# Half of the heads write their small products to the other rows of a second PSUM bank

## The chip, the cores and the metric

The kernel runs on one core of one Trainium2 chip. The metric is the device time of one execution, in microseconds (us); the time of a version is the median of its runs. The core's engines are TensorE (PE in the profile, its weight loads PEld), VectorE (DVE), ScalarE (ACT), GpSimd (POOL) and SyncE (SP), which issues the transfers.

## The reference

A delta-rule attention over 768 steps for 4 batches of 8 heads of width 48, and a feed-forward layer with a mish-like gate on its output.

```python
k_n = k / (np.linalg.norm(k, axis=-1, keepdims=True) + 1e-06)
for t in range(S):
    y[:, :, t] = einsum('bhd,bhde->bhe', q[:, :, t], state)
    v_old = einsum('bhde,bhd->bhe', state, k_n[:, :, t])
    state = state + beta[t] * einsum('bhd,bhe->bhde', k_n[:, :, t], v[:, :, t] - v_old)
x = y.transpose(0, 2, 1, 3).reshape(3072, 384)
h = x @ w_in                                  # 384 x 2048
g = h * np.tanh(np.log1p(np.exp(h)))          # h itself above 20
out = g @ w_out                               # 2048 x 384
```

## The kernel before

The 768 steps are cut into 12 chunks (n) of C = 64 steps. The 32 pairs of batch and head are 16 (NP) pairs p of two batch halves hh; hh = 0 and 1 lie on rows 0 to 63 and 64 to 127 of the tiles. The heads are also cut in two halves h of 8 (PB), and those in quarters h4 of four. Within a chunk the recurrence becomes matrix products: KK^T of the keys, the inverse T of a triangular 64x64 matrix made from it, Z~ = T times the values less K S, and y from Z~, Q and the state S.

Everything is written as stages, small Python generators, that are put on one plan with a time each (`put`, `at`, `defer`, and the table `TN`); the plan is run in order of these times. Up to plan time 90 the scheduler orders all engines; after it TensorE's instructions stay in the plan's order, and the scheduler orders the others. The stages on TensorE are:

- `early(g)`, for a group g of two chunks: the keys are transposed (kt, L267), KK^T goes to pg (L286), the masked part to d on VectorE (L289) and the rest to at on ScalarE (L291). VectorE then transposes d to gt (L297), makes the norms, and solves for the 32x32 diagonal blocks of T by 30 steps of two instructions each (pr at L345, gt at L347). In groups 0 and 1 16x16 blocks are solved, and `merge` joins them (ma, mb).
- `s_a` and `s_b` (ta, tb): the products of 32x32 blocks that give the off-diagonal block of T. Their copies go to at (L457) and tt (L473) on ScalarE.
- `s_gq` (gq): K S (48 columns) and K Q^T (64 columns) side by side, 64x64 weights. VectorE subtracts K S from the values vt (L488) and masks the rest into xx (L491).
- `s_z` (pz): Z~, 64x64 weights, 48 columns, copied to xx by ScalarE (L509).
- `s_y` (py, ps): the output y and the new state, with all 128 rows. `transposed` turns y into x for the feed-forward layer (xt), split into a high part (ScalarE, L561) and a low part (VectorE, L563).
- `moe(n)`: per chunk eight stages h (L586, x by w_in, 18 matmuls each) and eight acc (L615, 12 matmuls). Between them ScalarE and VectorE make g (L598, L599, L600). These stages lie between the attention stages on TensorE.

A matmul with 64 or 32 rows of weights and 64 or 32 columns occupies one tile of the PE array. Its rows are those of its operands, its columns those of the output's rows in PSUM. Before the change both follow hh alone: s_gq uses the tiles (rows 64 to 127, columns 0 to 63) and (rows 0 to 63, columns 64 to 127), s_z the other two, s_a and s_b two 32x32 tiles each, pg four of 64x32. A stage called with another (`at` with two stages) alternates with it matmul by matmul (`together`). The f32 matmuls take two passes each, so each is two instructions in the profile.

PSUM has eight banks: four in pool pa (tag "at", shared by all attention stages and the transposes), two for h and two for acc. The weights come as 64-bit floats, which ScalarE and VectorE convert in the first 150 us.

Of the kernel before, what the change touches and what calls it, by code (L numbers as in the profile page):

```python
# [3 lines left out]

# [6 lines left out]
F32 = mybir.dt.float32  # L11
# [4 lines left out]
ALU = mybir.AluOpType  # L16
# [19 lines left out]
def kernel(  # L36
# [22 lines left out]
    nc = tc.nc  # L59
# [126 lines left out]
    def load_w(parts):  # L186
        for n, (kind, i) in enumerate(parts):
# [68 lines left out]
    def early(g):  # L256
# [3 lines left out]
        for t2 in range(2):  # L260
            n = 2 * g + t2
            ks = srcs.get((g, t2), ksrc)
            if g > 1 and t2 == 0:
                load_src(ks, kk, n)
                yield
            kt = kts[n] = ap.tile([P, NP, 2, 32], F32, tag="kt", name=f"kt{n}", bufs=3)
            m = nc.vector.transpose(kt.rearrange("p a b c -> p (a b c)"), ks.rearrange("p a b c -> p (a b c)"))  # L267
            m
            if g > 1:
                tc.keep_in_program_order(m)  # L270
                if t2 == 0:
                    load_src(ks, kk, n + 1)
            yield
            at = ats[n] = ap.tile([P, NP, 32], F32, tag="at", name=f"at{n}", bufs=3)
            for h8 in range(2):
                tensor(1.05)
                ps = pa.tile([P, 8, C], F32, tag="at", name=f"pg{n}_{h8}")
                for p8 in range(8):
                    p = 8 * h8 + p8

                    for c in range(2):
                        for hh in range(2):
                            r = slice(64 - 64 * hh, 128 - 64 * hh)
                            r0 = 64 * hh + 32 * c
                            mv = kt[r, p] if c else kt[r, p, 0:1, :].broadcast_to([64, 2, 32])
                            nc.tensor.matmul(ps[r0:r0 + 32, p8, :], kt[r, p, c, :], mv, start=True, stop=True)  # L286

                def out(t2=t2, ps=ps, at=at, pr=slice(8 * h8, 8 * h8 + 8)):
                    nc.vector.tensor_tensor(out=dt[:, t2, pr, :], in0=ps[:, :, 32:],  # L289
                                            in1=bcast_mid(lmask, 8), op=ALU.mult)  # L290
# [143 lines left out]


    def together(*stages):
        for step in zip_longest(*stages):
            for f in step:
                if f is not None:
                    f()  # L440

    def mm(*a, then=None):
        def run():
            last[:] = [nc.tensor.matmul(*a, start=True, stop=True)]  # L444
            if then is not None:
                then()
        return run

    def s_a(n):

        at, tt = ats[n], tt2[:, n % 2]
        ps = pa.tile([P, NP, 32], F32, tag="at", name=f"ta{n}")

        def out():
            for hh in range(2):
                r = slice(64 * hh, 64 * hh + 32)
                nc.scalar.mul(out=at[r], in_=ps[r], mul=-1.0)  # L457

        for p in range(NP):
            for hh in range(2):  # L460
                r = slice(64 * hh + 32, 64 * hh + 64)
                yield mm(ps[64 * hh:64 * hh + 32, p, :], at[r, p, :], tt[r, p, 32:],
                         then=(lambda: defer(1.3, out)) if p == NP - 1 and hh else None)

    def s_b(n):

        at, tt, tn = ats[n], tt2[:, n % 2], tns[n // 2]
        ps = pa.tile([P, NP, 32], F32, tag="at", name=f"tb{n}")

        def out():  # L470
            for hh in range(2):
                r = slice(64 * hh, 64 * hh + 32)
                nc.scalar.copy(out=tt[r, :, 32:], in_=ps[r])  # L473

        for p in range(NP):
            for hh in range(2):
                r = slice(64 * hh, 64 * hh + 32)
                yield mm(ps[r, p, :], tn[r, n % 2, p, :], at[r, p, :], then=(lambda: defer(1.3, out)) if p == NP - 1 and hh else None)

    def s_gq(n, h):  # L480

        vt, x, kt = vts[n, h], xx[h], kts[n]

        d = D if n else 0
        def out(h4, ps):
            p4 = slice(4 * h4, 4 * h4 + 4)
            if n:
                nc.vector.tensor_tensor(out=vt[:, p4, :], in0=vt[:, p4, :], in1=ps[:, :, 0:D], op=ALU.subtract)  # L488
# [12 lines left out]

    def s_z(n, h):
        vt, x, tt = vts[n, h], xx[h], tt2[:, n % 2]
        pz = pa.tile([P, PB, D], F32, tag="at", name=f"pz{n}_{h}")

        def out():
            for hh in range(2):
                r = slice(64 * hh, 64 * hh + 64)
                nc.scalar.copy(out=x[r, :, hh, 0:D], in_=pz[r])  # L509

        for p in range(PB):
            for hh in range(2):
                r = slice(64 * hh, 64 * hh + 64)
                yield mm(pz[r, p, :], tt[r, PB * h + p, :], vt[r, p, :],
                         then=(lambda: defer(2.2 if n else 1.3, out)) if p == PB - 1 and hh else None)
# [251 lines left out]
    for g in range(1, NS // 2):  # L767
        n = 2 * g
# [58 lines left out]
```

## Time and profile before

| | |
|---|---|
| median of 3 runs | 688.57 us (687.88 to 689.55) |
| the profiled execution | 691.82 us |
| its span, from the first to the last instruction | 690.0 us |
| mean granted clock of TensorE | 0.94 |
| busy: PE, DVE, ACT, POOL | 633.7, 402.7, 273.9, 49.3 us |
| costliest groups on PE: h (L586), acc (L615) | 228.9 and 223.3 us |
| gq, py, ps, pz on PE | 43.8, 42.3, 38.4, 37.8 us |

Rows of instruction groups read: line, engine, operation, output <- inputs, (partitions x elements, type), xcount | busy time in us, mean ns of one | idle time of the engine ahead of them and what ended most of it. Rows of the timeline read: start in us, duration in us, engine, line, operation, names, shapes, xcount. A matmul's duration is from its start to its modelled end, so the time that a stage occupies TensorE is read from its first start to the start of the next stage.

### The profile page before, as it was taken

To read this page: it belongs to the slowest core of one execution; us is meant where nothing else is said; L and a number is where in the kernel's file an instruction comes from. 1 tells how busy PE (TensorE), PEld (TensorE's weight loads), DVE (VectorE), ACT (ScalarE), POOL (GpSimd) and SP (SyncE) were. 2 spreads that over 40 slices of the span, in tenths; PEclk is the share of its full clock that TensorE was granted. 3 is DMA by queue.
4 is the path that set the end of the run, shared out by engine and by line. 5 is a ranking of instruction groups with operands and counts; after the bars stand their busy time and mean duration, and the time that the engine had idled before them with its cause. 6 is when DMAs were issued, how large, how long until landed. Compare 5 with 4: busy or idle time off the path is not lost.

```text
span 690.0 us, 22887 instructions
## 1 busy us (share of the span) xinstructions
PE 633.7 (92%) x10163; PEld 584.7 (85%) x10163; DVE 402.7 (58%) x904; ACT 273.9 (40%) x521; POOL 49.3 (7%) x85
## 2 busy tenths in 40 slices
PE   5443799989988999999999999999999999999997
PEld 2213667769888999999999999999999999999997
DVE  4796268986147994369962499743799432321210
ACT  1350257644323333534435433344344353433331
POOL 5011000100100002000010010020000200000000
PEclk9565579999899999999999999999999999999999
DMA  5896721022132340231322402321222021010001
GB/s 81 208 257 115 287 44 30 2 34 42 22 62 35 48 71 18 44 61 31 44 57 36 69 17 41 66 39 22 48 37 47 13 37 37 12 25 2 1 24 24
DMA packets 160931, 37.76 MB, mean 55 GB/s; under 512 B 154176, under 2 KB 157248, under 8 KB 160832
## 3 DMA queue, kind: packets, MB, share of 16 engines
q1 hardware_dynamic: 160832, 36.30, 26.8%
q8 instruction: 80, 1.31, 0.8%
q14 instruction: 19, 0.16, 0.1%
HBM read 31.56 MB, written 4.72 MB: 53 GB/s over the span
## 4 chain that ended last, share of the span: by engine, by line
PE 82%; SPq 7%; DVE 5%; issue 3%; DMA 2%; ACT 1%; POOL 0%; DVEq 0%; ACTq 0%; POOLq 0%
PE h L586 30%; PE acc L615 29%; SPq L171 7%; PE gq L444 5%; PE py L444 4%; PE ps L444 2%; PE pg L286 2%; PE pz L444 2%; PE tb L444 2%; PE ta L444 2%; PE xt L559 1%; PE loi L241 1%; DMA ksrc<-in_k_dram 1%; PE ma L386 1%; PE mb L397 1%
## 5 line engine op out<-in xcount | busy, mean ns | idle before, releaser
L586 PE MATMUL h<-x,wi 128*128 128x256 f32 x1728 | 228.9, 287 | 0.6 <-DVE x L563 0.6
L615 PE MATMUL acc<-wo,g 128*128 128x384 f32 x1152 | 223.3, 343 | 0.0
L586 PEld LDWEIGHTS h<-x,wi 128*128 128x128 f32 x1728 | 217.1, 191 | 4.9 <-issue 0.8
L615 PEld LDWEIGHTS acc<-wo,g 128*128 128x128 f32 x1152 | 200.3, 190 | 3.4 <-issue 0.3
L600 DVE TENSOR_TENSOR g<-e,g 128x512 fp32r<-128x512 f32 x96 | 66.2, 690 | 172.2 <-ACT g L599 171.9
L598 ACT ACTIVATE e<-h 128x512 f32<-128x512 f32 x96 | 57.3, 597 | 195.1 <-PE h L586 189.0
L599 ACT CAST g<-e 128x512 fp32r<-128x512 f32 x96 | 59.5, 620 | 3.0
L345 DVE TENSOR_TENSOR pr<-gt 128x84 f32<-128x84 f32 (+14 forms) x148 | 47.8, 323 | 3.9
L347 DVE TENSOR_TENSOR gt<-gt,pr 128x84 f32<-128x84 f32 (+14 forms) x148 | 47.4, 321 | 3.9
L444 PE MATMUL gq<-xx,kt 64*64 64x112 f32 (+1 forms) x768 | 43.8, 266 | 1.6 <-ACT wo L246 1.6
L432 DVE STREAM_TRANSPOSE xx<-qsrc 64x512 f32<-64x512 f32 x48 | 33.8, 705 | 19.0 <-PE ps L444 14.6
L444 PEld LDWEIGHTS py<-xx 128*64 128x64 f32 x768 | 38.5, 141 | 6.7 <-issue 5.8
L491 DVE TENSOR_TENSOR xx<-gq,amask 64x256 f32<-64x256 f32 x96 | 40.2, 419 | 5.2 <-PE gq L444 4.4
L444 PE MATMUL py<-xx 128*64 128x48 f32 x768 | 42.3, 228 | 0.0
L425 POOL TENSOR_TENSOR vt<-vt,ne 128x384 f32<-128x384 f32 x24 | 20.5, 858 | 296.1 <-DMA vt<-in_v_dram 138.2
L444 PEld LDWEIGHTS gq<-xx,kt 64*64 64x64 f32 x768 | 38.0, 141 | 3.4 <-ACT wo L246 1.8
L444 PE MATMUL pz<-vt,tt 64*64 64x48 f32 x768 | 37.8, 236 | 1.9 <-issue 1.2
L444 PEld LDWEIGHTS pz<-vt,tt 64*64 64x64 f32 x768 | 34.5, 140 | 4.8 <-issue 2.4
L444 PE MATMUL ps<-xx 128*48 128x48 f32 x704 | 38.4, 211 | 0.0
L509 ACT COPY xx<-pz 64x384 f32<-64x384 f32 x48 | 22.7, 474 | 35.0 <-PE gq L444 29.3
L444 PEld LDWEIGHTS ps<-xx 128*48 128x48 f32 x704 | 31.8, 128 | 0.0
L286 PEld LDWEIGHTS pg<-kt 64*32 64x32 f32 x1536 | 23.0, 109 | 7.3 <-issue 5.4
(111 smaller groups left out, 575.4 us busy)
## 6 DMA issues: line engine op xcount, KB each, us to landing
ri<-in_moe_w_in_dram SPq DMA_DIRECT2D x12, 512.0 KB, 5.3
ro<-in_moe_w_out_dram SPq DMA_DIRECT2D x16, 384.0 KB, 5.9
vt<-in_v_dram SPq DMA_DIRECT2D x48, 96.0 KB, 2.6
xx<-in_k_dram SPq DMA_DIRECT2D x48, 96.0 KB, 2.9
out_dram<-o SPq DMA_DIRECT2D x48, 96.0 KB, 2.5
qsrc<-in_q_dram SPq DMA_DIRECT2D x48, 64.0 KB, 2.7
ksrc<-in_k_dram SPq DMA_DIRECT2D x44, 64.0 KB, 2.7
qsrc<-in_q_dram SPq DMA_DIRECT2D x48, 32.0 KB
```

The lines of the kernel that those rows point to most:

```text
L171: m = nc.sync.dma_start(out=dst, in_=src)
L286: nc.tensor.matmul(ps[r0:r0 + 32, p8, :], kt[r, p, c, :], mv, start=True, stop=True)
L345: nc.vector.tensor_tensor(out=pv, in0=nj, in1=xj, op=ALU.mult)
L347: nc.vector.tensor_tensor(out=below, in0=below, in1=pv, op=ALU.add)
L432: nc.vector.transpose(xx[h][r, :, hh, D:D + C], src)
L444: last[:] = [nc.tensor.matmul(*a, start=True, stop=True)]
L491: nc.vector.tensor_tensor(out=x[r, p4, hh, D:D + C], in0=ps[r, :, d:], in1=bcast_mid(amask[r], 4), op=ALU.mult)
L586: nc.tensor.matmul(h[:, f2, :], wt["i", f * P // WI * NCH + c][:, i2, f0:f0 + P], x[:, c, :], start=(i == 0), stop=(i == 3 * NCH - 1))
L598: for d, f in ((0.7, lambda: nc.scalar.activation(e, h, AF.Mish, scale=-1.0)), (0.7, lambda: nc.scalar.copy(out=gg[:, 0], in_=e)), (0.8, l ...
L599: (0.7, lambda: nc.scalar.copy(out=gg[:, 0], in_=e)),
L600: (0.8, lambda: nc.vector.tensor_tensor(out=gg[:, 1], in0=e, in1=gg[:, 0], op=ALU.subtract))):
L615: nc.tensor.matmul(acc[t], gg[:, a, f2, ts_], wt["o", f][:, i2, :], start=(f == 0 and i == 0), stop=(f == NF - 1 and i == 2))
```

## The change

Each stage's heads are divided in two: one part writes its output to the rows it used before, the other part to rows shifted by 64 (pg, gq, pz) or by 32 (ta, tb). So twice as many tiles of the PE array are used: four for gq, pz, ta or tb, eight for pg and for tb together with ta. The shifted part of gq, pz and pg has a PSUM bank of its own (pz takes two banks where it took one). Reading PSUM, the copies and the VectorE operations on the shifted part go from one set of rows to another, and those that took all 128 rows at once are split into two (`sides`). The number of matmuls is unchanged.

Per chunk, ScalarE's copies go from two to four for each pz, for ta and for tb, and from two to three for pg. VectorE's masks on d go from two to three, and its subtractions from vt from two to three for each half of the heads; the masks on gq stay at four. `together` now takes four matmuls of a stage before it changes to the other. Plan times of some copies move by a few tenths.

```diff
+    def sides(crossed):
+        if not crossed:
+            return [(slice(0, P), slice(0, P))]
+        return [(slice(64 * i, 64 * i + 64), slice(64 - 64 * i, 128 - 64 * i)) for i in range(2)]
...
             for h8 in range(2):
-                tensor(1.05)
-                ps = pa.tile([P, 8, C], F32, tag="at", name=f"pg{n}_{h8}")
-                for p8 in range(8):
-                    for c in range(2):
-                        for hh in range(2):
...
-                            r0 = 64 * hh + 32 * c
...
+            pg = [pa.tile([P, 8, C], F32, tag="at", name=f"pg{n}_{h8}") for h8 in range(2)]
+            for p8 in range(8):
+                for c in range(2):
+                    for h8 in range(2):
+                        for hh in range(2):
+                            r0 = 64 * (hh ^ h8) + 32 * c
...
+            def out(h8, t2=t2, pg=pg, at=at):
+                pr, ps = slice(8 * h8, 8 * h8 + 8), pg[h8]
+                for r, i in sides(h8):
+                    nc.vector.tensor_tensor(out=dt[r, t2, pr, :], in0=ps[i, :, 32:],
+                                            in1=bcast_mid(lmask[i], 8), op=ALU.mult)
+                for r, i in sides(h8):
+                    nc.scalar.copy(out=at[r, pr, :], in_=ps[i, :, 0:32])
...
     def together(*stages):
-        for step in zip_longest(*stages):
-            for f in step:
-                if f is not None:
-                    f()
+        todo = [list(f) for f in stages]
+        for i in range(0, max(map(len, todo)), 4):
+            for f in todo:
+                for step in f[i:i + 4]:
+                    step()
...
     def s_a(n):
...
+        def out(pr):
+            for hh in range(2):
+                i = 64 * hh + 32 * (pr.start > 0)
+                nc.scalar.mul(out=at[64 * hh:64 * hh + 32, pr], in_=ps[i:i + 32, pr], mul=-1.0)
+        for p in halves():
+            for hh in range(2):
+                r = slice(64 * hh + 32, 64 * hh + 64)
+                i = 64 * hh + 32 * (p // PB)
+                yield mm(ps[i:i + 32, p, :], at[r, p, :], tt[r, p, 32:],
...
     def s_gq(n, h):
...
+                for r, i in sides(h4):
+                    nc.vector.tensor_tensor(out=vt[r, p4, :], in0=vt[r, p4, :], in1=ps[i, :, 0:D], op=ALU.subtract)
             for hh in range(2):
                 r = slice(64 * hh, 64 * hh + 64)
+                i = slice(64 * (hh ^ h4), 64 * (hh ^ h4) + 64)
+                nc.vector.tensor_tensor(out=x[r, p4, hh, D:D + C], in0=ps[i, :, d:],
+                                        in1=bcast_mid(amask[i], 4), op=ALU.mult)
+        pg = [pa.tile([P, 4, C + d], F32, tag="at", name=f"gq{n}_{h}{h4}") for h4 in range(2)]
+        for p in range(4):
+            for h4 in range(2):
                 for hh in range(2):
                     r = slice(64 - 64 * hh, 128 - 64 * hh)
+                    i = slice(64 * (hh ^ h4), 64 * (hh ^ h4) + 64)
+                    yield mm(pg[h4][i, p, :], kt[r, PB * h + 4 * h4 + p], x[r, 4 * h4 + p, hh, D - d:D + C],
...
     def s_z(n, h):
+        pz = [pa.tile([P, 4, D], F32, tag="at", name=f"pz{n}_{h}{h4}") for h4 in range(2)]
...
+                nc.scalar.copy(out=x[r, 4 * h4:4 * h4 + 4, hh, 0:D], in_=pz[h4][i])
```

`s_b` changes as `s_a` does. Lines move down: pg is L291 after, d L296, the substitution L355 and L357, the stages' matmuls L456, x's low part L592, h L615, g L629 and acc L644.

How the rows stand on TensorE, first at a KK^T stage of the last group, between a stage h and a stage acc. Names carry the program's tile numbers; x2 means two equal rows in a row. Before:

```order
L586 MATMUL h_2_7059<-x_7_6762,wi_1080 128x256
L586 MATMUL h_2_7059<-x_7_6763,wi_1080 128x256
L586 MATMUL h_2_7059<-x_7_6762,wi_1080 128x256
L286 MATMUL pg_0_7081<-kt_6978 32x64 x32
L286 MATMUL pg_1_7114<-kt_6978 32x64 x32
L615 MATMUL acc_7_7157<-wo_567,g_0_6905 128x384 x3
```

After:

```order
L615 MATMUL h_2_7186<-x_7_6881,wi_1094 128x256
L615 MATMUL h_2_7186<-x_7_6882,wi_1094 128x256
L615 MATMUL h_2_7186<-x_7_6881,wi_1094 128x256
L291 MATMUL pg_0_7208<-kt_7105 32x64 x2
L291 MATMUL pg_1_7209<-kt_7105 32x64 x2
L291 MATMUL pg_0_7208<-kt_7105 32x64 x2
L291 MATMUL pg_1_7209<-kt_7105 32x64 x2
```

The stage stays between the same h and acc; the two banks alternate every two matmuls instead of following each other.

The second place is a stage of pz with gq on TensorE. Before:

```order
L444 MATMUL pz_1_6530<-vt_1_5553,tt_106 64x48
L444 MATMUL gq_00_6531<-xx_98,kt_4837 64x112
L444 MATMUL pz_1_6530<-vt_1_5553,tt_106 64x48
L444 MATMUL gq_00_6531<-xx_98,kt_4837 64x112
L444 MATMUL pz_1_6530<-vt_1_5553,tt_106 64x48
```

After:

```order
L456 MATMUL pz_10_6643<-vt_1_5652,tt_106 64x48 x2
L456 MATMUL pz_11_6644<-vt_1_5652,tt_106 64x48 x2
L456 MATMUL gq_00_6645<-xx_98,kt_4920 64x112 x2
L456 MATMUL gq_01_6646<-xx_98,kt_4920 64x112 x2
L456 MATMUL pz_10_6643<-vt_1_5652,tt_106 64x48 x2
```

Four matmuls of pz, two to each bank, are now followed by four of gq. 

The third place is VectorE near the end of the substitution of group 4, where x of chunk 6 is made; pr and gt are a step's product and sum. Before:

```order
L345 TENSOR_TENSOR pr_16_6135<-gt_5773 128x240
L600 TENSOR_TENSOR g_6_6056<-e_6_6055,g_6_6056 128x512
L347 TENSOR_TENSOR gt_5773<-gt_5773,pr_16_6135 128x15x16
L345 TENSOR_TENSOR pr_17_6152<-gt_5773 128x238
L563 TENSOR_TENSOR x_6_6079<-xt_0_6080,x_6_6078 128x3x128
L347 TENSOR_TENSOR gt_5773<-gt_5773,pr_17_6152 128x14x17
L563 TENSOR_TENSOR x_6_6079<-xt_1_6084,x_6_6078 128x3x128
L345 TENSOR_TENSOR pr_18_6176<-gt_5773 128x234
```

After:

```order
L355 TENSOR_TENSOR pr_16_6242<-gt_5874 128x240
L357 TENSOR_TENSOR gt_5874<-gt_5874,pr_16_6242 128x15x16
L629 TENSOR_TENSOR g_6_6163<-e_6_6162,g_6_6163 128x512
L355 TENSOR_TENSOR pr_17_6259<-gt_5874 128x238
L357 TENSOR_TENSOR gt_5874<-gt_5874,pr_17_6259 128x14x17
L592 TENSOR_TENSOR x_6_6186<-xt_0_6187,x_6_6185 128x3x128
L355 TENSOR_TENSOR pr_18_6283<-gt_5874 128x234
L592 TENSOR_TENSOR x_6_6186<-xt_1_6191,x_6_6185 128x3x128
L357 TENSOR_TENSOR gt_5874<-gt_5874,pr_18_6283 128x13x18
```

The second half of x_6 now stands behind one more instruction of the substitution.

More of the change, by code (lines that the diff above doesn't have):

```diff
@@ L2 @@
 from heapq import heappop, heappush
-from itertools import zip_longest
 import concourse.bass as bass
@@ L447, in mm, with halves, both @@
         return run
+    def halves():
+        return [PB * i + p for p in range(PB) for i in range(2)]
+    def both(t, out):
+        for i in range(2):
+            defer(t + 0.4 * i, out, slice(PB * i, PB * i + PB))
     def s_a(n):
@@ L452, in s_a @@
         ps = pa.tile([P, NP, 32], F32, tag="at", name=f"ta{n}")
-        def out():
+        def out(pr):
             for hh in range(2):
-                r = slice(64 * hh, 64 * hh + 32)
-                nc.scalar.mul(out=at[r], in_=ps[r], mul=-1.0)
-        for p in range(NP):
+                i = 64 * hh + 32 * (pr.start > 0)
+                nc.scalar.mul(out=at[64 * hh:64 * hh + 32, pr], in_=ps[i:i + 32, pr], mul=-1.0)
+        for p in halves():
             for hh in range(2):
                 r = slice(64 * hh + 32, 64 * hh + 64)
-                yield mm(ps[64 * hh:64 * hh + 32, p, :], at[r, p, :], tt[r, p, 32:],
-                         then=(lambda: defer(1.3, out)) if p == NP - 1 and hh else None)
+                i = 64 * hh + 32 * (p // PB)
+                yield mm(ps[i:i + 32, p, :], at[r, p, :], tt[r, p, 32:],
+                         then=(lambda: both(1.2, out)) if p == NP - 1 and hh else None)
     def s_b(n):
@@ L468, in s_b, with out @@
         ps = pa.tile([P, NP, 32], F32, tag="at", name=f"tb{n}")
-        def out():
+        def out(pr):
+            for hh in range(2):
+                i = 64 * hh + 32 * (pr.start > 0)
+                nc.scalar.copy(out=tt[64 * hh:64 * hh + 32, pr, 32:], in_=ps[i:i + 32, pr])
+        for p in halves():
             for hh in range(2):
                 r = slice(64 * hh, 64 * hh + 32)
[L473 to L478, printed above, removed]
+                i = 64 * hh + 32 * (p // PB)
+                yield mm(ps[i:i + 32, p, :], tn[r, n % 2, p, :], at[r, p, :],
+                         then=(lambda: both(1.2, out)) if p == NP - 1 and hh else None)
     def s_gq(n, h):
@@ L487, in out @@
             if n:
-                nc.vector.tensor_tensor(out=vt[:, p4, :], in0=vt[:, p4, :], in1=ps[:, :, 0:D], op=ALU.subtract)
+                for r, i in sides(h4):
+                    nc.vector.tensor_tensor(out=vt[r, p4, :], in0=vt[r, p4, :], in1=ps[i, :, 0:D], op=ALU.subtract)
             for hh in range(2):
                 r = slice(64 * hh, 64 * hh + 64)
-                nc.vector.tensor_tensor(out=x[r, p4, hh, D:D + C], in0=ps[r, :, d:],
-                                              in1=bcast_mid(amask[r], 4), op=ALU.mult)
@@ L494, in s_gq @@
-        for h4 in range(2):
-            ps = pa.tile([P, 4, C + d], F32, tag="at", name=f"gq{n}_{h}{h4}")
-            for p in range(4):
+                i = slice(64 * (hh ^ h4), 64 * (hh ^ h4) + 64)
[4 more added lines that the diff above has]
+            for h4 in range(2):
@@ L497, in s_gq @@
                 for hh in range(2):
                     r = slice(64 - 64 * hh, 128 - 64 * hh)
-                    yield mm(ps[64 * hh:64 * hh + 64, p, :], kt[r, PB * h + 4 * h4 + p], x[r, 4 * h4 + p, hh, D - d:D + C],
-                             then=(lambda h4=h4, ps=ps: defer(1.2 + h4, out, h4, ps)) if p == 3 and hh else None)
+                    i = slice(64 * (hh ^ h4), 64 * (hh ^ h4) + 64)
+                    yield mm(pg[h4][i, p, :], kt[r, PB * h + 4 * h4 + p], x[r, 4 * h4 + p, hh, D - d:D + C],
+                             then=(lambda h4=h4: defer(1.2 + h4, out, h4, pg[h4])) if p == 3 and hh else None)
@@ L502, in s_z, with out @@
     def s_z(n, h):
         vt, x, tt = vts[n, h], xx[h], tt2[:, n % 2]
-        pz = pa.tile([P, PB, D], F32, tag="at", name=f"pz{n}_{h}")
-        def out():
+        pz = [pa.tile([P, 4, D], F32, tag="at", name=f"pz{n}_{h}{h4}") for h4 in range(2)]
+        def out(h4):
             for hh in range(2):
                 r = slice(64 * hh, 64 * hh + 64)
[L509 to L515, printed above, removed]
+                i = slice(64 * (hh ^ h4), 64 * (hh ^ h4) + 64)
+                nc.scalar.copy(out=x[r, 4 * h4:4 * h4 + 4, hh, 0:D], in_=pz[h4][i])
@@ L517, in s_y @@
+        for p in range(4):
+            for h4 in range(2):
+                for hh in range(2):
+                    r = slice(64 * hh, 64 * hh + 64)
+                    i = slice(64 * (hh ^ h4), 64 * (hh ^ h4) + 64)
+                    yield mm(pz[h4][i, p, :], tt[r, PB * h + 4 * h4 + p, :], vt[r, 4 * h4 + p, :],
+                             then=(lambda h4=h4: defer((2.0 if n else 1.2) + 0.4 * h4, out, h4)) if p == 3 and hh else None)
     def s_y(n, h):
```

18 lines of the change are left out of this document (8 added, 10 removed).

## The prediction

> **What bounds the kernel now.** I read the totals of the page first, then the shares of the chain that ended last, then busy time by stretch, then what TensorE waits for, and last the instructions of single stages.
>
> ```profile
> PE 633.7 (92%) x10163; PEld 584.7 (85%) x10163; DVE 402.7 (58%) x904; ACT 273.9 (40%) x521; POOL 49.3 (7%) x85
> PE 82%; SPq 7%; DVE 5%; issue 3%; DMA 2%; ACT 1%; POOL 0%; DVEq 0%; ACTq 0%; POOLq 0%
> ...
> 194.00:690.00 496.00, 488.57 (x7375) 470.80 (x7373) 277.39 (x605) 194.74 (x362) 26.27 (x38) 1.00 0.22 37
> 393.65:424.90 31.25, 31.25 (x489) 30.24 (x489) 28.14 (x72) 12.35 (x23) 1.82 (x3) 1.00 0.23 40
> 424.90:486.73 61.83, 61.83 (x1030) 59.21 (x1029) 34.92 (x69) 26.04 (x49) 4.43 (x6) 1.00 0.25 44
> 55.00:70.00 15.00, 6.27 (x301) 5.90 (x301) 9.27 (x22) 0.55 (x2) 3.36 (x6) 0.50 0.61 139
> 100.00:125.00 25.00, 24.27 (x528) 18.85 (x526) 22.03 (x49) 19.20 (x39) 0.00 (x0) 1.00 0.24 37
> ...
> PE pg L286 <- issue: 1.9, 1, 1.9
> PE pg L286 <- DVE kt L267: 1.0, 1, 1.0
> ```
>
> A row of a stretch gives its length, then busy time of PE, PEld, DVE, ACT and POOL, the clock, DMA share and GB/s. The last two rows are all that PE waits for after 200 us: 2.9 us. So from 194 us on PE is the bound at clock 1.00, and what shortens its stream shortens the end until something else is late. The chance of that is read from the second and third stretch: from pg of an odd chunk to the first h of the next even chunk (31.25 us) DVE is busy for 28.14 us, since the substitution on gt (L345, L347) runs there; in the 61.83 us after it, for 34.92. The front is another matter: at 55 to 70 us the clock is 0.50, and in 100 to 125 us DVE is busy for 22.03 of 25.
>
> **What a pass on a tile costs.** An f32 matmul is two passes, each an instruction of a row's xcount. The first and the following stage's row give each stage's length.
>
> ```profile
> 393.65 1.99 PE L286 MATMUL pg<-kt 64*32 64x64 f32 x128
> 395.57 0.80 PE L615 MATMUL acc<-wo,g 128*128 128x384 f32 x3
> ...
> 447.96 0.25 PE L444 MATMUL pz<-vt,tt 64*64 64x48 f32 x1
> ...
> 448.97 0.26 PE L444 MATMUL gq<-xx,kt 64*64 64x112 f32 x1
> ...
> 449.07 0.26 PE L444 MATMUL gq<-xx,kt 64*64 64x112 f32 x1
> ...
> 449.65 1.57 PE L586 MATMUL h<-x,wi 128*128 128x256 f32 x11
> ...
> 462.47 1.20 PE L444 MATMUL ta<-tt,at 32*32 32x32 f32 x64
> 463.60 0.63 PE L615 MATMUL acc<-wo,g 128*128 128x384 f32 x2
> ...
> 468.71 0.21 PE L444 MATMUL tb<-at,tn 32*32 32x32 f32 x1
> ...
> 469.92 0.79 PE L615 MATMUL acc<-wo,g 128*128 128x384 f32 x3
> ...
> 627.09 1.14 PE L444 MATMUL pz<-vt,tt 64*64 64x48 f32 x32
> 628.15 0.62 PE L586 MATMUL h<-x,wi 128*128 128x256 f32 x3
> ...
> 436.01 0.29 PE L444 MATMUL py<-xx 128*64 128x48 f32 x4
> ...
> 436.22 0.29 PE L444 MATMUL py<-xx 128*64 128x48 f32 x4
> ```
>
> - pg: 1.92 us, 128 passes on four tiles, 32 on each. Less 0.13 us of run-in (my estimate from the stages' first rows) that is 56 ns a pass and tile.
> - pz with gq: 1.69 us. pz has two tiles, gq two others, 16 passes each; gq's come back every 0.10 us (448.97, 449.07), and 16 of these (1.53 at 95.6 ns) fill the stage. pz alone: 1.06 us for 16 passes a tile, 59 ns, so beside gq its two tiles idle for a third of the time.
> - ta: 1.13 us, 32 passes on each of two tiles, 32 ns a pass. tb with ta: 1.21 us, 128 passes on four tiles, so PE takes one every 8.6 ns there.
> - py and ps: eight passes in 0.21 us (436.01 to 436.22), 26 ns each, though all use the same 128 rows and only the columns differ. So tiles of the same rows do run beside each other.
>
> **The change on PE.** No instruction is added; the passes of a stage are spread over twice the tiles.
>
> - pz with gq: each of four tiles gets 8 passes of pz and 8 of gq: 8 x 59 + 8 x 95.6 = 1.24 us in place of 1.53, -0.29 a stage. From 194 us there are 18 (576 gq passes by 32): -5.2. pz alone, once: 8 x 59 in place of 16, -0.47.
> - ta or tb alone: 16 passes a tile, 0.51 by the tiles; 64 x 8.6 = 0.55 by the closest spacing seen. I take 0.55 and 0.11 of run-in, 0.66: -0.47. Ten of them: -4.7.
> - tb with ta goes to eight tiles: 0.55 by the tiles if passes may follow each other at 4.3 ns, 1.10 if 8.6 ns is the limit. So 0 to -0.55 each; I take -0.2, near the measured spacing, for four: -0.8.
> - pg: 16 passes a tile, 0.90; by the spacing 1.10. With the run-in 1.03 to 1.23; I take 1.12, -0.8. Eight after 194 us, of which the one at 205 us waits (the 1.9 and 1.0 above) and gets nothing: -5.6.
>
> The sum of PE's part from 194 us is -16.8 us. Where two stages alternate, the turn is now four matmuls and not one. Those four meet four different tiles, so no tile is hit twice in a row, and I cost it at nothing.
>
> By the Trainium skill (TensorE: Matmul & The Clock Gate, Part 3: Packing small matmuls) a weight load overlaps matmuls in flight only where the row group differs. The new tiles lie in row groups already in use, so by that sentence PE's part would be about 0 and not -16.8. The py and ps rows speak against it here: 26 ns a pass in one row group.
>
> **The change on ACT and DVE.** Where half of the heads sit in other rows, a copy is split.
>
> ```profile
> L509 ACT COPY xx<-pz 64x384 f32<-64x384 f32 x48 | 22.7, 474 | 35.0 <-PE gq L444 29.3 <-PE pz L444 5.2
> L533 ACT COPY xx<-ps 48x384 f32<-48x384 f32 x44 | 20.9, 474 | 0.8
> L536 ACT COPY yy<-py 128x384 f32<-128x384 f32 x24 | 11.5, 478 | 39.4 <-PE ps L444 34.7 <-PE py L444 4.7
> L457 ACT ACTIVATE at<-ta 32x512 f32<-32x512 f32 x24 | 14.1, 586 | 11.1 <-PE ta L444 10.8
> L488 DVE TENSOR_TENSOR vt<-vt,gq 128x192 f32<-128x192 f32 x44 | 15.5, 352 | 8.3 <-PE gq L444 7.6
> L289 DVE TENSOR_TENSOR d<-pg,lmask 128x256 f32<-128x256 f32 x24 | 9.5, 418 | 7.8 <-PE pg L286 7.6
> L345 DVE TENSOR_TENSOR pr<-gt 128x240 f32<-128x240 f32 x8 | 3.3, 408 | 0.2
> ```
>
> ACT: 128 columns less (586 to 474) save 112 ns, 0.875 ns a column. So 192 columns cost about 306 ns and 256 about 362. pz: per chunk and half four of 306 for two of 474, +276 ns x 24 = 6.6 us. ta and tb: (4 x 362 - 2 x 586) x 24 = 6.6. pg's copies go from 24 to 36, at 0.37: 4.4. Together +18 us on an engine idle for 416: off the path, hidden by PE's stages between one copy and its reader. DVE: d 24 to 36, +12 x 0.42 = 5.0; vt 44 to 66, +22 x 0.35 = 7.7. The masks on gq stay 96. None of before's rows moves data between rows, so the price of that is open: from nothing to a doubling of the extra pieces, which would add another 13 us on DVE. I take nothing more: 48, 64 and 128 rows of 384 columns take 474, 474 and 478 ns, so the columns have set the time and not the rows. A stage of pz with gq now holds four banks of the pool instead of three, all that it has. The stage at 447.96 ends at 449.65, its copies (0.3 to 0.5 us each, two or four in a row on an engine) some 3 us later, and up to ta at 462.47 only one other attention stage (py) needs the pool, so I cost that at nothing; with the cover gone it would be about 1 us a stage, 18 in all. SP and POOL get nothing added.
>
> **Where the gain stops.** In the 31.25 us half-period (the third pair below) and the three like it the end of DVE's work is this:
>
> ```profile
> 395.04 0.69 DVE L600 TENSOR_TENSOR g<-e,g 128x512 fp32r<-128x512 f32 x1 [2.27 <-ACT g L599]
> 395.76 0.76 DVE L289 TENSOR_TENSOR d<-pg,lmask 128x256 f32<-128x256 f32 x2
> ...
> 238.15 0.55 DVE L563 TENSOR_TENSOR x<-xt,x 128x384 fp32r<-128x384 f32 x1
> 238.63 1.10 PE L586 MATMUL h<-x,wi 128*128 128x256 f32 x7
> 330.61 0.55 DVE L563 TENSOR_TENSOR x<-xt,x 128x384 fp32r<-128x384 f32 x1
> 331.83 1.35 PE L586 MATMUL h<-x,wi 128*128 128x256 f32 x10
> 423.76 0.55 DVE L563 TENSOR_TENSOR x<-xt,x 128x384 fp32r<-128x384 f32 x1
> ...
> 424.90 2.29 PE L586 MATMUL h<-x,wi 128*128 128x256 f32 x18
> 516.80 0.55 DVE L563 TENSOR_TENSOR x<-xt,x 128x384 fp32r<-128x384 f32 x1
> 517.97 2.29 PE L586 MATMUL h<-x,wi 128*128 128x256 f32 x18
> ```
>
> In chunk 6 x is ready at 424.31 and h starts at 424.90: 0.59 us of slack after 28.6 us of nearly unbroken DVE work, whose start (d) follows g, which an earlier pg doesn't move. The chain gets one more d (0.38), one more vt (0.35), and by the order one more step of the substitution ahead of x_6's second half (0.41): +1.14 us. So x comes at 425.45, 0.55 later than h starts now, while PE is through with its own work some 1.6 us earlier (pg 0.8, pz with gq 0.29, tb 0.47). h then waits 2.1 us for x, and this half-period is 0.5 us longer than before instead of 1.6 shorter. The same reading gives the four (h of chunks 2, 4, 6, 8) slacks of -0.07, 0.67, 0.59 and 0.62 us. Chunk 4 has the same step more and gets +0.5 too. At 8 the order has two steps fewer ahead of x (-0.8), which cancels the added pieces; h can use its slack, -0.7. At 2 it has four more (+1.6), but on this first turn DVE also waits for PE, whose work comes sooner: between +2.3 and -0.9 I take the middle, +0.7. Sum of the four: +0.7 + 0.5 + 0.5 - 0.7 = +1.0.
>
> The three 61.8 us half-periods have DVE idle for 27 us, so PE's gain stays: 3 pz with gq 0.87, pg 0.8, ta 0.47, tb with ta 0.2, that is -2.3 each, -6.9. The stretch from 518 us to the end has no substitution: five pz with gq, one pz alone, two single ta or tb, one pair, -3.1. From 150 to 194 us four stages have waits beside them: -0.8 out of some 1.5. Before that the attention stages run at half clock on the first chunk's chain, which would be worth more, but PE is busy 6.27 of 15 us at 55 to 70 and DVE's conversions hold 100 to 125: I take -1.4, with bounds +2 and -6.
>
> Sum: +1.0 - 6.9 - 3.1 - 0.8 - 1.4 = -11.2 us. The profiled execution took 691.82 us (span 690.0 and 1.8 around it), 3.25 above the median of 688.57; the saving is taken from the median: 677.4 us.
>
> **The rivals.**
> - All of PE's gain arrives: if DVE's small gaps in the half-period shrink (28.14 of 31.25, so 3.1 us are there), or the earlier stages let g and d start sooner, x keeps pace. Then -16.8 - 0.8 - 1.4 = -19.0: 669.6. Against it: d follows g at 395.76, and g doesn't come from pg. 20%.
> - Passes can't be issued closer than some 8.6 ns, or more than four tiles don't fill: pg and single ta or tb get half, tb with ta nothing. Half-periods with substitution stay +1.0 (x sets them), the others -1.4 each, the end -2.2, the front -1.0: -6.4, 682.2. 12%.
> - Slower: the added tiles share rows with others and don't overlap with them. PE keeps its time, and each half-period with substitution gets DVE's added 1.1 us less its slack: about +1.2 at 2 (half of 2.3), +0.5 each at 4 and 6, 0 at 8; +2.2, 690.8. It decides from the point where stages save less than some 0.3 us per half-period. py and ps speak against it. 5%. (The rule of the Trainium skill named above would have this result.)
> - Nothing measurable: stage gains of a third, eaten by x. 3%.
>
> **How the numbers follow.** My forecast gets 60%, with a range of its own from 672 to 682 (the front's bounds and the pg and ta spacing). 669.6 gets 20%, 682.2 12%, 690.8 5%, no change 3%. The range from 668 to 684 leaves out the last two and the outer part of the first rival, about 15% in all. About 0.2% (1.4 us) is what a measurement of this kernel can tell from no change. Faster: 0.60 + 0.20 + 0.12 = 0.92; same 0.03; slower 0.05.
>
> **What would show it.** Right, step by step: pg near 1.1 us, pz with gq near 1.40, ta near 0.66, with PE waits of about 2 us each for x (DVE L592 in the new numbering) ahead of h of chunks 4 and 6, and PE busy time after 200 us down by some 16 us. Wrong: stages that keep their length (the slower rival), or stages that shrink with no wait for x (the full gain), d or vt pieces longer than 0.42 us (moving between rows costs), waits of PE for a free bank at tb or gq, or issue waits at the denser stages.

## The result, and the profile after

The changed kernel took 682.44 us in the median of 4 runs (680.29 to 684.27), against 689.06 for the kernel before in the same series: ratio 0.990, 95% interval 0.986 to 0.994, so 6.6 us faster. The forecast was 677.4. The profiled execution took 680.29 us, its span is 678.6. Ratios here and below compare fast executions alone: one of the changed kernel (686.58 us, in experiment 1) fell in a slower state and counts in its median and range only.

The lines of the page after and of its views that answer to those of before: totals, the chain's shares, the same three stretches (the half-period before chunk 6, the one after it, and the steady part), and what PE waits for after 200 us.

```profile
PE 611.0 (90%) x10163; PEld 560.8 (83%) x10163; DVE 413.1 (61%) x938; ACT 292.4 (43%) x629; POOL 50.1 (7%) x85
PE 78%; DVE 6%; ACT 2%; issue 2%; SPq 1%; DMA 0%; DVEq 0%; ACTq 0%
...
194.00:678.00 484.00, 472.18 (x7223) 453.87 (x7222) 283.68 (x627) 207.49 (x442) 25.34 (x36) 0.99 0.22 37
386.90:417.60 30.70, 30.70 (x494) 29.56 (x493) 27.00 (x69) 13.31 (x28) 1.92 (x3) 1.00 0.23 38
417.60:478.70 61.10, 59.61 (x1025) 56.85 (x1025) 38.59 (x78) 28.17 (x62) 4.42 (x6) 1.00 0.28 47
...
PE h L615 <- DVE x L592: 3.7, 3, 1.5
PE pg L291 <- issue: 2.1, 1, 2.1
PE pg L291 <- DVE kt L272: 1.1, 1, 1.1
```

The row from 194 us on doesn't hold the same work as before's: the changed kernel is further on at that time, and the row counts 7223 matmuls against 7375. So the difference of the two (488.57 to 472.18, 16.4 us) is not what the change saves on PE. From the first h of chunk 2 to the end the work is equal, before first:

```profile
238.64:690.00 451.36, 446.79 (x6479) 431.09 (x6478) 245.38 (x528) 178.12 (x330) 23.22 (x33) 1.00 0.20 35
234.50:678.50 444.00, 435.76 (x6479) 419.31 (x6478) 252.88 (x551) 190.28 (x404) 23.32 (x33) 1.00 0.21 36
```

There PE has 11.0 us less to do and DVE 7.5 more. The wait for x is new: part of the gain has turned into it.

The stages, in the timeline of PE (the first row of a stage, then that of the stage behind it):

```profile
387.49 1.59 PE L291 MATMUL pg<-kt 64*32 64x64 f32 x128
389.01 0.45 PE L644 MATMUL acc<-wo,g 128*128 128x384 f32 x1
...
421.62 0.33 PE L456 MATMUL pz<-vt,tt 64*64 64x48 f32 x8
...
423.01 0.44 PE L644 MATMUL acc<-wo,g 128*128 128x384 f32 x1
...
455.86 0.75 PE L456 MATMUL ta<-tt,at 32*32 32x32 f32 x64
456.55 0.62 PE L644 MATMUL acc<-wo,g 128*128 128x384 f32 x2
...
461.64 0.23 PE L456 MATMUL tb<-at,tn 32*32 32x32 f32 x4
...
462.86 0.44 PE L644 MATMUL acc<-wo,g 128*128 128x384 f32 x1
```

pz with gq is down from 1.69 to 1.39 us, ta from 1.13 to 0.69, pg from 1.92 to 1.52 here and 1.41 at its shortest; tb with ta stays at 1.22. Added up from the first h of chunk 2 on, from each stage's first start to the next stage's: pz with gq 28.80 to 23.70 (17 stages), pg 11.52 to 8.84 (6), ta and tb alone 9.04 to 5.46 (8), pz alone 1.06 to 0.61, tb with ta 4.87 to 4.86 (4). That is 11.8 us. h, whose work is unchanged, goes from 177.23 to 181.75: 4.5 us more, around the three waits for x.

### The profile page after: what moved, and what is told of

The parts are those of the page before. It is cut to its first block, busy times and chain, and to the rows that moved or that the text cites. A ratio compares the mean times of both kernels' runs of the same rounds, so it can differ in the third digit from the quotient of the medians.

```text
span 678.6 us, 23070 instructions
## 1 busy us (share of the span) xinstructions
PE 611.0 (90%) x10163; PEld 560.8 (83%) x10163; DVE 413.1 (61%) x938; ACT 292.4 (43%) x629; POOL 50.1 (7%) x85
## 4 chain that ended last, share of the span: by engine, by line
PE 78%; DVE 6%; ACT 2%; issue 2%; SPq 1%; DMA 0%; DVEq 0%; ACTq 0%
PE h L615 30%; PE acc L644 29%; PE py L456 4%; PE gq L456 2%; PE ps L456 2%; PE pz L456 2%; PE pg L291 2%; PE loi L246 1%; PE tb L456 1%; PE ta L456 1%; PE xt L588 1%; PE loo L246 1%; PE ma L396 1%; DVE gt L357 1%; DVE pr L355 1%
## 5 line engine op out<-in xcount | busy, mean ns | idle before, releaser
L615 PE MATMUL h<-x,wi 128*128 128x256 f32 x1728 | 227.7, 285 | 4.3 <-DVE x L592 4.3
L615 PEld LDWEIGHTS h<-x,wi 128*128 128x128 f32 x1728 | 215.4, 189 | 9.2 <-DVE x L592 5.3
L644 PE MATMUL acc<-wo,g 128*128 128x384 f32 x1152 | 222.0, 341 | 0.8 <-issue 0.8
L644 PEld LDWEIGHTS acc<-wo,g 128*128 128x128 f32 x1152 | 199.3, 189 | 4.3 <-issue 1.3
L629 DVE TENSOR_TENSOR g<-e,g 128x512 fp32r<-128x512 f32 x96 | 66.0, 687 | 152.9 <-ACT g L628 152.8
L355 DVE TENSOR_TENSOR pr<-gt 128x84 f32<-128x84 f32 (+14 forms) x148 | 47.2, 319 | 3.9
L357 DVE TENSOR_TENSOR gt<-gt,pr 128x84 f32<-128x84 f32 (+14 forms) x148 | 46.6, 315 | 3.9
L456 PEld LDWEIGHTS py<-xx 128*64 128x64 f32 x768 | 39.4, 144 | 6.6 <-issue 4.9
L435 POOL TENSOR_TENSOR vt<-vt,ne 128x384 f32<-128x384 f32 x24 | 22.0, 922 | 302.5 <-DMA vt<-in_v_dram 114.3
L456 PE MATMUL py<-xx 128*64 128x48 f32 x768 | 43.5, 231 | 0.0
L456 PE MATMUL ps<-xx 128*48 128x48 f32 x704 | 39.4, 214 | 0.0
L536 ACT COPY xx<-pz 64x192 f32<-64x192 f32 x96 | 30.1, 314 | 19.0 <-PE pz L456 17.8
L456 PE MATMUL gq<-xx,kt 64*64 64x112 f32 (+1 forms) x768 | 33.0, 269 | 1.0 <-ACT wo L251 0.6
L456 PEld LDWEIGHTS ps<-xx 128*48 128x48 f32 x704 | 32.5, 131 | 0.0
L456 PE MATMUL pz<-vt,tt 64*64 64x48 f32 x768 | 28.5, 225 | 1.4 <-issue 0.9
L565 ACT COPY yy<-py 128x384 f32<-128x384 f32 x24 | 11.5, 479 | 39.8 <-PE ps L456 25.9
L456 PEld LDWEIGHTS pz<-vt,tt 64*64 64x64 f32 x768 | 23.5, 139 | 5.7 <-issue 3.5
L246 PE MATMUL loi<-mi,ident 128*128 128x512 f32 x18 | 13.6, 846 | 14.9 <-DVE mi L235 14.3
```

What stands on the lines that cost most here:

```text
L246: nc.tensor.matmul(ps, ident, a, start=True, stop=False)
L355: nc.vector.tensor_tensor(out=pv, in0=nj, in1=xj, op=ALU.mult)
L357: nc.vector.tensor_tensor(out=below, in0=below, in1=pv, op=ALU.add)
L536: nc.scalar.copy(out=x[r, 4 * h4:4 * h4 + 4, hh, 0:D], in_=pz[h4][i])
L615: nc.tensor.matmul(h[:, f2, :], wt["i", f * P // WI * NCH + c][:, i2, f0:f0 + P], x[:, c, :], start=(i == 0), stop=(i == 3 * NCH - 1))
L629: (0.8, lambda: nc.vector.tensor_tensor(out=gg[:, 1], in0=e, in1=gg[:, 0], op=ALU.subtract))):
```

## The experiments

All times are of several executions, each with its interval; the kernel before ran beside each set, with medians of 687.3, 688.4 and 688.0 us.

**1. The changed kernel once more.**

> The changed kernel once more, to size its gain: its profiled execution saved 11.5 us against that of before, its median only 6.6. If the steady part (from the second chunk's first h on) carries the gain, the stretch from that h to the end is again about 11 us shorter than before's, and executions differ in the front alone, where loads and conversions set the pace: median 680 to 684, ratio 0.985 to 0.993. If the profiled pair was lucky in the steady part, that stretch comes out 2 us or more longer this time.

Median 680.97 us of 6 runs (676.35 to 686.58), ratio 0.9904, interval 0.987 to 0.9938; over all ten runs the median is 681.4. From the moment when x of chunk 2 is ready (and its h can run on) to the end, the first profile takes 442.4 us and this one 443.0; before's takes 451.3. So the steady gain is 8.3 to 8.9 us and repeats; the executions differ ahead of that point. By the expectation's own measure, from the first h of chunk 1, the two profiles also agree (505.9 us, against 516.9 of before), but experiment 2 shows that 3.6 us of that difference belong to one execution of before.

**2. The kernel before once more**, for the same reason.

> The kernel before once more, for a second profile. If the steady part is as fixed as in the changed kernel (506.0 twice), the stretch from the first h of chunk 1 to the end is 516.8 again within 0.5 us and the front alone differs from 173.2: near 169, which the median of its times asks for.

688.61 us, ratio 1.0013 (0.9981 to 1.0045). From x of chunk 2 to the end it is 451.3 us again, to a tenth. But the point comes at 234.0 us and not at 238.7, so the expectation picked the wrong place: the first h of chunk 1 is at 172.0 against 173.2, and 3.5 us arise between there and chunk 2. The clock row and one stretch (length, PE, PEld, DVE, ACT, POOL, clock), of the first profile of before and then of this one:

```profile
PEclk9565579999899999999999999999999999999999
175.00:200.00 25.00, 22.87 (x641) 20.91 (x642) 7.04 (x14) 7.85 (x16) 3.25 (x5) 0.82 0.15 27
```

```profile
PEclk9565579999999999999999999999999999999999
175.00:200.00 25.00, 21.89 (x724) 19.89 (x712) 8.91 (x17) 9.19 (x19) 2.93 (x5) 1.00 0.24 44
```

Between 175 and 200 us the same program had a mean clock of 0.82 in one execution and 1.00 in the other; 0.18 of 25 us is 4.5 us of full speed, which covers the 3.5 us. The profile from which the forecast was made had such a front. This also gives a way to size the front without a profile: the median time less 1.75 us around the span less the fixed rest. For before that is 688.0 - 1.75 - 451.3 = 235.0 us up to x of chunk 2; for the changed kernel 681.4 - 1.75 - 442.7 = 237.0. It holds where the clock behind that point is 1.00, as it is in these profiles; in experiments 3 and 4 it is not.

**3. The tiles alone undone.**

```diff
-                            r0 = 64 * (hh ^ h8) + 32 * c
+                            r0 = 64 * hh + 32 * c
...
```

Likewise for gq, pz, ta and tb, and for the rows that are read (`sides`); the split copies, second banks, turns and plan times stay.

> The changed kernel with all products in the old rows (only the tiles are undone; split copies, second banks, turns of four and plan times stay). If the tiles carry the gain, stages return to 1.69 (pz with gq), 1.13 (ta, tb) and 1.92 us (pg), x is still late by about 0.5 us for h of chunks 4 and 6, and the time is 1 to 3 us over before: 690 to 692. If the split copies cost more than their columns say, over 694. If the gain comes from the turns or the plan times, it stays near 682.

706.05 us, ratio 1.0281 (1.0255 to 1.0307). The stages are back at 1.71 (pz with gq), 1.13 and 1.94 us, so the tiles are what shortens them. The rest of the expectation failed: x isn't late for chunks 4 to 8 (slack 1.35 us). The rest from x of chunk 2 on is only 3.5 us longer than before (454.8), and 2.5 of these come from a clock of 0.50 between 248.8 and 254.5 us, in which an h and a pz with gq took that much longer. But the front is 14.5 us longer by difference (706.05 - 1.75 - 454.8 = 249.5), or 17 with the rest taken at full clock. One wait stands out:

```profile
PE h L615 <- DVE x L592: 6.7, 2, 6.1
```

6.1 us of it are h of chunk 2 waiting for x. What this kernel keeps of the change costs far more in the front than the columns of the split copies say; whether the copies, the second banks or the plan times do it is not shown here.

**4. pg as before in the changed kernel, and 5. pg alone in the kernel before.**

```diff
-            pg = [pa.tile([P, 8, C], F32, tag="at", name=f"pg{n}_{h8}") for h8 in range(2)]
...
+            for h8 in range(2):
+                tensor(1.05)
+                ps = pa.tile([P, 8, C], F32, tag="at", name=f"pg{n}_{h8}")
...
```

Minus is both banks at once on eight tiles, plus is bank by bank on four; experiment 5 makes the step the other way, from the kernel before.

> The changed kernel with KK^T (pg) as before: four tiles, one mask on d per bank. If x on VectorE sets the half-periods with the substitution, a pg longer by 0.5 us is hidden there and d is one piece shorter: +0.5 in each of the three other half-periods, -0.3 in each of the four, within 1.5 us of the changed kernel, 681 to 684. If stage lengths add up, 7 x 0.5 and the two of the front on top: 686.

> The kernel before with pg alone on eight tiles and its split d. pg should be about 1.41 us. If x sets the half-periods with the substitution, their 0.6 us of slack is used up by the extra d (0.4), so they gain at most 0.1 to 0.5 each and the others 0.5: -2 to -3, 686 to 687. If d's extra piece makes x late there: about 688.

Without the new pg: 685.69 us, ratio 0.9976 (0.9954 to 0.9998). From x of chunk 2 on it took 444.8 us, 2.1 longer than with it. But most of that isn't pg's. A row of this stretch, and h of chunk 2 behind x with the stage after it, in this kernel and then in the changed one:

```profile
242.30:245.70 3.40, 3.40 (x30) 3.18 (x32) 3.16 (x10) 0.37 (x1) 0.00 (x0) 0.50 0.00 0
```

```profile
241.74 3.56 PE L610 MATMUL h<-x,wi 128*128 128x256 f32 x17 [3.20 <-DVE x L587]
245.22 0.47 PE L451 MATMUL pz<-vt,tt 64*64 64x48 f32 x8
```

```profile
236.27 2.29 PE L615 MATMUL h<-x,wi 128*128 128x256 f32 x17 [1.50 <-DVE x L592]
238.49 0.33 PE L456 MATMUL pz<-vt,tt 64*64 64x48 f32 x8
```

At a clock of 0.50 the same 17 passes took 3.48 us in place of 2.22, and the stage behind them 1.6 in place of 1.39: 1.5 us. That leaves some 0.6 of the 2.7 us by which pg's stages are longer; the rest of these is hidden, as expected, and the waits for x before chunks 4 and 6 are 0.3 us each in place of 0.8 and 1.5. The median still lies over the range expected for that, and on the 686 of the other branch: by difference the front is 685.69 - 1.75 - 443.3 = 240.6, 3.6 longer than the changed kernel's, and why it is stays open. With pg alone: 693.14 us, ratio 1.0092 (1.0061 to 1.0123), slower than before. Its rest is 448.7, that is -2.6, as expected; its front is 693.14 - 1.75 - 448.7 = 242.7, that is +7.7, which no theory of mine had.

**6. The change from chunk 2 on only, and 7. in chunks 0 and 1 only.** The old and the new functions stand side by side and are chosen by chunk, pg by group: the early part of pg is groups 0 and 1, that is chunks 0 to 3.

```diff
     def s_gq(n, h):
+
+        if n >= 2:
+            yield from s_gq_new(n, h)
+            return
...
```

This is experiment 6; experiment 7 has `n < 2`.

> The change from chunk 2 on only; chunks 0 and 1 (their pg, gq, pz, ta, tb and copies) stay as before, so every engine's order is the old one up to about 170 us. Theory: from the first h of chunk 1 to the end the change saves 10.8 us in both profiles of it (516.8 to 506.0), and some 4.5 us are given back in the front, where VectorE and ScalarE convert weights and get the added copies. Then this saves nearly all of the 10.8: 676 to 679, ratio 0.983 to 0.988. Rival: the front's 4.5 us are chance, or come from the later part: as the changed kernel, 680 to 682.

> The change in chunks 0 and 1 only. By the theory the front is longer by about 4.5 us in the median and the rest as before (516.8 us from the first h of chunk 1): 690 to 693, slower than before by 0.3 to 0.8%. Rival (the front gains, as the prediction had it, by 1.4 us): 686.

From chunk 2 on only: 678.33 us, ratio 0.9859 (0.982 to 0.9898), as expected. Its rest is 441.4, its front 678.33 - 1.75 - 441.4 = 235.2, that of before. From the first h of chunk 2 on VectorE is busy about as long as in the changed kernel (252.1 and 252.9 us), and yet x is ready 0.33 and 0.36 us ahead of h of chunks 4 and 6, with 16 steps of the substitution ahead of it in place of 18; only in chunk 8 does h wait for it (1.6 us). In the front only: 694.84 us, ratio 1.0105 (1.0064 to 1.0145), slower, and by more than the 690 to 693 expected. Its rest is 451.3 to the tenth, its front 241.8. So the same edit gains 10 us in the later chunks and loses 6.8 in the first ones. That the two don't add up to the changed kernel's front of 237.0 suggests that the loss depends on what else is placed there.

**8. pg on eight tiles in chunks 0 to 3 only**, the rest as before.

> The kernel before with pg on eight tiles in chunks 0 to 3 only (four more masks on d, four more copies; two banks filled at once). If the front's loss is the added work on VectorE and ScalarE, 4 x 0.4 us: 689 to 690. If it is the order in which the front's conversions and these stages are placed (only pg: 693.1, of which the later chunks give 2.6 back), 693 to 697.

694.6 us, ratio 1.0107 (1.0071 to 1.0142): pg alone brings a loss as large as that of experiment 7. Four extra masks on d of 0.42 us are 1.7 us and don't explain 6.5. Waits of PE between 100 and 172 us, of this kernel first, then of before (its second profile):

```profile
PE loo L247 <- ACT wo L252: 4.1, 1, 4.1
PE loi L247 <- DVE mi L236: 1.7, 1, 1.7
PE pg L293 <- ACT at L301: 0.7, 1, 0.7
...
PE gq L477 <- ACT at L301: 0.5, 1, 0.5
```

```profile
PE loi L241 <- DVE pr L345: 2.5, 1, 2.5
PE gq L444 <- ACT wo L246: 1.6, 1, 1.6
```

loi and loo are matmuls in the conversion of the weights, wo and mi its steps on ACT and DVE. They wait longer, and pg and gq now wait for the copies at that free a bank of pool pa: the two banks of pg are taken at once, beside those of the conversions. The waits of before have no such entry. These waits of PE add up to 8.4 us in this stretch, against 5.4 in before's second profile. Two more parts stand beside these 3 us: h of chunk 2 waits 2.0 us for x here and not at all there, and the clock between 125 and 150 us is 0.86 against 0.93, 1.7 us of full speed. That the placement and the banks do it, and not the amount of work, fits the size but was not separated, neither from each other nor from the clock.

**9. The substitution's second pg planned one h and one acc earlier**, on top of experiment 6.

```diff
-... gg=(-4.05,-3.85,-3.692,-3.691,-2.85,-2.692,-2.691), ...
+... gg=(-4.05,-3.85,-3.692,-3.691,-2.91,-2.755,-2.754), ...
...
-                                            *spread(-2.6, TN['sg'], 30 if g < FG else 63), -1.43)))
+                                            *spread(-2.6 - 0.06 * (g > 2), TN['sg'] - 0.06 * (g > 2), 30 if g < FG else 63), -1.43)))
```

> The change from chunk 2 on only, and the second pg of groups 3 to 5 with its substitution planned one h and one acc (some 4.4 us) earlier. If x on VectorE is what holds h of chunks 4 and 6 by 1 to 1.7 us each, these waits go (1.5 to 4 us less than the kernel without the move): 672 to 676. If the substitution's own dependencies or g set x, the waits stay and so does the time.

682.32 us, ratio 0.9915 (0.9882 to 0.9948): 4 us slower than experiment 6, with a rest of 447.2. The expectation went by the waits of the changed kernel; experiment 6, on which this one builds, had none at chunks 4 and 6 to take away. The start of the substitution moved, and so did its order against x: 22 and 23 of its steps now run ahead of x of chunks 6 and 8, in place of 16 and 18. x came 1.8 and 2.0 us late for these, and a new wait appeared at py:

```profile
PE h L728 <- DVE x L705: 3.3, 2, 1.7
PE py L485 <- issue: 3.1, 3, 1.4
```

**10. x put ahead in VectorE's order, in the changed kernel, and 11. the same on top of experiment 6.** In the changed kernel x runs long after it could. The timelines of ACT (high part of x), DVE (low part) and PE before chunk 6:

```profile
413.24 0.86 ACT L590 CAST x<-xt 128x384 fp32r<-128x384 f32 x2 [1.19 <-PE xt L588]
...
418.00 0.55 DVE L592 TENSOR_TENSOR x<-xt,x 128x384 fp32r<-128x384 f32 x1
418.47 0.39 DVE L355 TENSOR_TENSOR pr<-gt 128x234 f32<-128x234 f32 x1
418.78 0.55 DVE L592 TENSOR_TENSOR x<-xt,x 128x384 fp32r<-128x384 f32 x1
...
417.61 0.28 PE L615 MATMUL h<-x,wi 128*128 128x256 f32 x1
419.38 0.86 PE L615 MATMUL h<-x,wi 128*128 128x256 f32 x5 [1.49 <-DVE x L592]
```

Its inputs are there at 414.10; it runs at 418.00 and 418.78 behind the substitution, and h, which has done one pass with the high part at 417.61, goes on at 419.38. The edit gives the steps of the substitution that the plan has behind x a dependency on it.

```diff
+            m = nc.vector.tensor_tensor(out=pv, in0=nj, in1=xj, op=ALU.mult)
+            if g >= 2 and xlow and xlow[0] == 2 * g - 2:
+                order(m, xlow[1])
...
```

Here m is the product pr of a step and xlow x's low part. Experiment 11 has `g >= 3`, which leaves x of chunk 2 out.

> The changed kernel with one more rule of order on VectorE: steps of the substitution that the plan has behind x's low part also stand behind it (x_6 8 rows earlier). x's inputs lie ready 3.5 to 4.3 us before it runs in the changed kernel, so if its place in VectorE's order holds h, the waits of h of chunks 2, 4 and 6 (1.7, 1.0, 1.7 us) go and the time falls by 3 to 5 us, to 676 to 678.5. If the half-periods with the substitution are bound by VectorE's amount of work, the wait comes back elsewhere (g or tt late) and the time stays near 681.

> The change from chunk 2 on only, with the same rule of order. There h waits for x in chunk 8 alone (1.85 us), so 1 to 2 us less than the 678.3 measured without the rule: 676 to 677.5, ratio 0.981 to 0.985, the best of all versions. If VectorE's work binds: 678.

The changed kernel with the rule: 675.95 us, ratio 0.983 (0.980 to 0.986), 5.4 us below the changed kernel. On top of experiment 6: 675.99 us, ratio 0.9819 (0.9786 to 0.9851). These are the best two, and they don't differ, though only the first has the change in the front too. The first of them, its DVE and PE before chunk 6, and its waits of PE after 200 us:

```profile
415.96 1.00 DVE L596 TENSOR_TENSOR x<-xt,x 128x384 fp32r<-128x384 f32 x2
...
418.88 2.29 PE L621 MATMUL h<-x,wi 128*128 128x256 f32 x18
...
PE pg L291 <- issue: 2.4, 1, 2.4
PE pg L291 <- DVE kt L272: 2.1, 1, 2.1
PE acc L650 <- issue: 0.7, 1, 0.7
```

x is done 1.9 us ahead of h and no wait for x is left; the rest from x of chunk 2 is 439.9, 11.4 below before's. Added up as above, its stages are 11.3 us shorter than before's, so all that they gain arrives. VectorE's amount of work was not the bound: its order was. Its front by difference is 675.95 - 1.75 - 439.9 = 234.3, since the wait for x of chunk 2 (1.7 and 2.1 us in the two profiles of the changed kernel) has gone too.

**12. Turns of one in place of four in the changed kernel.**

> The changed kernel with stages alternating matmul by matmul as before, in place of turns of four. If PE runs ahead over the tiles, the turn is without effect: pz with gq 1.39 us, 679 to 684. If the turns are what fills the four tiles, pz with gq returns towards 1.53 to 1.69 and the time rises by 3 to 6 us.

679.26 us, ratio 0.9872 (0.9841 to 0.9904), and pz with gq takes 1.39 us: the turn of four has no effect on the stage. Experiment 3 nearly agrees: there four matmuls in a row fall on two tiles, and pz with gq takes 1.71 us for 1.69, tb with ta 1.32 for 1.22. That the median is lower than the changed kernel's goes with x again: x of chunk 6 isn't late here, and the rest is 440.9.

## Why the prediction was right, and where its sizes were off

- *Tiles of the same rows run beside each other.* Right: -0.30 for pz with gq (forecast -0.29), -0.45 for ta or tb alone (-0.47), -0.45 for pz alone (-0.47). The rule of the Trainium skill that the prediction weighed (TensorE: Matmul & The Clock Gate, Part 3: Packing small matmuls), that a weight load overlaps matmuls in flight only in other row groups, would have left these stages as they were; the trace disagrees.
- *The spacing of passes.* pg gained 0.4 to 0.5 and not 0.8: its 128 passes start 10 to 11 ns apart and not 8.6. tb with ta on eight tiles still starts a pass every 8.6 ns, so its -0.2 was 0. Together 2.9 us too much: the three half-periods without the substitution gained 1.85 each and not 2.3, and pg didn't come near the 1.1 us that the prediction named as its sign.
- *Copies.* ACT +18.5 us (forecast +18). DVE +10.4 (+12.7). Moving between rows costs nothing that shows: experiment 3, with the same split and no crossing, also has 352 ns for the 64 rows of vt. The pieces of d and vt that cross (64 rows) and those that don't (128 rows):

```profile
L512 DVE TENSOR_TENSOR vt<-vt,gq 64x192 f32<-64x192 f32 x44 | 15.5, 352 | 0.6
L512 DVE TENSOR_TENSOR vt<-vt,gq 128x192 f32<-128x192 f32 x22 | 7.6, 346 | 3.9 <-PE gq L456 3.9
L296 DVE TENSOR_TENSOR d<-pg,lmask 64x256 f32<-64x256 f32 x24 | 10.1, 422 | 0.5
L296 DVE TENSOR_TENSOR d<-pg,lmask 128x256 f32<-128x256 f32 x12 | 5.0, 416 | 3.8 <-PE pg L291 3.7
```

- *x late in the half-periods with the substitution.* Right in place and size: before chunk 6 the stretch from pg to x ready is 387.49 to 419.33, 31.84 us, where before pg to h took 31.25: +0.6, forecast +0.5. Before chunk 4 it is 0.0 and +0.5 in the two profiles (+0.5), before chunk 8 -1.2 (-0.7). The waits of h are 0.8 to 1.5 us and not 2, since PE's own stages there gain about 1.15 and not 1.6. Experiments 6 and 10 show the cause, with one correction: the half-period wasn't full, x stood too far back in it. Part of the rival with the full gain was to be had by a rule of order: 5.4 us, 2.8 of them behind x of chunk 2.
- *From chunk 2 on.* The terms (+0.5 + 0.5 - 0.7 - 6.9 - 3.1 = -9.7) against 451.3 to 442.7: -8.6. The prediction named PE's busy time as a sign, some 16 us less after 200 us; for equal work it is 11.0.
- *The front.* This is the term that was mis-sized. Forecast: -1.4 up to 150 us, -0.8 to 194, +0.7 at chunk 2, that is -1.5. Measured by difference: 235.0 to 237.0, +2.0, with medians that vary by about a microsecond. 3.5 of the 4.6 us missing (11.2 forecast, 6.6 measured) lie here. x of chunk 2 comes 1.7 and 2.1 us behind the start of its h in the two profiles; without that the front is as long as before. So the -2.2 counted up to there came to nothing, and the +0.7 for this x to 1.7 to 2.1. Experiments 7 and 8 show that the change alone can lose 6.5 to 6.8 us there, and experiment 10 that the wait for x of chunk 2 is the larger part of what was left in the changed kernel. The likeliest value had the wrong sign. It counted shorter stages on PE, where the waits of experiment 8 point to the conversions on DVE and ACT.
- *The clock, a rival not shut out.* The mean granted clock on record is 0.947 over 55 executions of the kernel before, 0.941 over ten of the changed kernel, 0.940 in experiment 5 and 0.942 in experiments 7 and 8. 0.006 of 680 us is 4 us of full speed, more than the front's loss in the changed kernel. Against it stands experiment 6, which has 0.942 too and the front of before. Whether the change lowers the clock, and what that costs, was not tested.
- *Luck.* The median of 682.44 lies just outside the 672 to 682 that the likeliest value had for itself, and on the number of the second rival (682.2). That is partly chance: pg got about half of its gain and tb with ta none, as this rival had it, but the single ta and tb got nearly all of theirs, and it is the front that brings the time there.

What stays open is how the new pg delays the front: by its two banks at a time, by the order on ACT and DVE that follows from it, or by the clock.

## What to carry to other kernels

Small matmuls that share rows but not columns did run side by side here, and where PE was the bound writing them to the other rows of a second bank cost only the split copies; look for the closest spacing of passes in the trace before more than four tiles are paid for. When the engine that is relieved starts to wait, compare when the late operand's inputs were ready with when it ran: here 3.9 us lay between, and one rule of order was worth about as much as the change itself. Try such a change also on only the stretch where that engine is the bound: without the rule of order it lost elsewhere part of what it gained there, and with the rule the two versions didn't differ. Before two stretches of time are compared, see that they hold the same instructions and had the same clock.

## What the runs showed of the hardware

In one set of 19 executions the kernel before took 684.88 to 693.73 us, and its two profiles put their difference ahead of chunk 2: a granted clock of 0.82 against 1.00 between 175 and 200 us, with 451.3 us both times for all that follows. A sum that is read from one profile carries that. The later stretch isn't always free of it: in experiment 4 the clock was 0.50 from 242.3 to 245.7 us, and 17 passes of h took 3.48 us for 2.22.

Reading PSUM on 64 rows and writing the other 64 took VectorE no longer than staying on the same rows: 352 ns for 192 columns with the crossing and without it (experiment 3). The passes of tb with ta came no closer than some 8.6 ns on eight tiles, the spacing that they had on four.
